# Attention by key chunks of 128, with the leftover 64 keys of two head pairs in one shared slot

## The chip, the cores and the metric

The kernel runs on one core of one Trainium2 chip. The metric is the device time in microseconds (us) of one execution. The engines' short names are those of the profile: PE (matrix multiply, TensorE), PEld (its weight loads), DVE (VectorE), ACT (ScalarE), POOL (GpSimd) and SP (SyncE, which mostly issues DMA transfers).

## The reference

Attention with normalized queries and keys is followed by a feed-forward block with a squared ReLU. There are 8 batches, 12 heads, 448 rows a head and 64 numbers a row; everything is float32.

```python
q_n, k_n = rmsnorm(q, g_q), rmsnorm(k, g_k)          # over the 64 numbers of a row
scores = matmul(q_n, k_n.T) / sqrt(64)
attn = exp(scores - max(scores)); attn = attn / (sum(attn) + 1e-9)
x = matmul(attn, v)                                   # then (B,H,S,D) -> (B*S, H*D): 3584 x 768
h = maximum(x @ w_in, 0)                              # w_in 768 x 2048
out = (h * h) @ w_out                                 # w_out 2048 x 768
```

## The kernel before

**Pairs, chunks and visits.** Two heads make a pair, and their 2 x 64 numbers fill the 128 rows of the array. There are 48 pairs, six to a batch. The 448 keys of a pair are cut into NJ = 4 chunks of 112. For a chunk `weigh` (L312 on) multiplies the chunk's keys with all 448 queries, for each head on its own half of the array's rows (L327). ACT takes the exponential into a tile `wT` (L329), with the key's 1/rms as its scale. `attend` (L366 on) multiplies `wT` with the values, each head on its own half of the array's columns (L372). A visit (`visit`, `weigh_chunks`) attends two chunks of the pair before and weighs two chunks of this pair. So a pair has two visits and a unit of two batches has 24.

**Denominators.** For the first two batches (`alone(i)`) the sums of the weights come from a matmul with ones after each chunk (L379). For the later ones POOL adds the four chunks' weights (`add_up`, L340), and one matmul with ones a pair (`denominators`, L387) sums over the keys. Then DVE inverts (L406) and multiplies (`finish`, L415). The result `xT` is a piece of the transposed x.

**Queries and keys.** `Rows` loads them (L120), squares them on ACT (L133), sums on DVE (L138, L141), takes the power -1/2 on POOL (L147) and scales the queries (L163). For the first 14 pairs PE transposes them (`turn`, L307). For later ones (`in_blocks`) the queries go out to memory and come back in blocks of 32 x 32 (`store_q`, `load_blocks`), and DVE transposes the blocks (L264). Up to batch 1 a row's place in its tile is "(p j)": chunk j holds the rows 4p + j. From batch 2 on the keys and values are "(j p)". `store` writes output rows in the same two orders, so a tile of 128 rows often leaves in pieces.

**Feed-forward part.** It works on units of two batches, with a seven-product scheme for a 2 x 2 block product. `first_products` (L520, 448 columns) makes h; DVE adds (L540), and ACT applies ReLU and square (L541, L542). `second_products` (L572 and L601, 384 columns) makes the output, which DVE adds up in `acc` (L642). The combinations of x that it needs are made by `make_x_forms` (L442) on DVE and POOL, once both batches' pairs are there. The weights are converted piece by piece in the first stage and in unit 0 (`convert`; L710 to L712, L723 to L751).

**Order.** The order in which instructions are issued on every engine is written out by hand (`manual_schedule`). In the first stage (`visit_alone`) attention runs with no feed-forward work between. From then on `ffn(u)` is a generator with a cost for every product, and `run` works through it until a given share is spent; between two such runs stands a visit (`visit_among`). So each unit's feed-forward part has the attention of a later unit between its products. The last unit runs bare. Small jobs wait in `tasks` (DVE) and `pool_tasks` (POOL) and are issued one or two after each product.

**PSUM banks.** There are eight. Scores use banks 0 to 3, two chunks deep; values use bank 4 (4 and 5 in the first two batches). Denominators use 6 and 7 in the first two batches and bank 3 after them. The feed-forward part has 5 to 7.

Of the kernel before, what the change touches and what calls it, by code (L numbers as in the profile page):

```python
# [21 lines left out]
P = 128  # L22


NJ = 4
BY_ROW = "p j"

IN_ORDER = "j p"
# [8 lines left out]
MOST_G = 7.5  # L37


@with_exitstack  # L40
def kernel(
# [19 lines left out]
    CP = q.shape[2] // NJ  # L61
    const = ctx.enter_context(tc.tile_pool(name="const", bufs=1))
    ident = const.tile([P, P], F32, name="ident")
    ones = const.tile([CP, D], F32, name="ones")
    minus_half = const.tile([CP, 1], F32, name="minus_half")
# [4 lines left out]
    with tc.tile_pool(name="early", bufs=1) as early, tc.manual_schedule(engines=ENGINES):  # L70
        for n, g in enumerate((g_q, g_k)):
            nc.scalar.dma_start(g_rows[:, n], g.rearrange("(one d) -> one d", one=1))
        rows.load(0, (nc.sync, nc.scalar))
# [11 lines left out]
        rows.normalize_first(0, early)  # L85
# [5 lines left out]


class Rows:


    def __init__(self, nc, pools, q, k, ones, minus_half):
        self.nc, self.pools, self.qk = nc, pools, (q, k)
        self.ones, self.minus_half = ones, minus_half
        self.B, self.H, self.S, self.D = q.shape
        self.CP = self.S // NJ  # L100
        self.tiles, self.squares, self.ms, self.rr = {}, {}, {}, {}
        self.room = {}

    def go_on(self, io, small):

        other = copy(self)
        other.pools = SimpleNamespace(io=io, small=small)
        other.tiles, other.rr = dict(self.tiles), dict(self.rr)
        return other

    def new_tile(self):
        return self.pools.io.tile([P, 2, 2 * NJ, self.D], F32, name="qk", tag="qk")

    def load(self, i, queues, orders=(BY_ROW, BY_ROW)):
        b, c = divmod(i, self.H // 2)
        self.room[i] = self.new_tile()
        qk = self.room[i][: self.CP]
        for x, rows in enumerate(self.qk):
            for e in range(2):
                queues[x].dma_start(  # L120
                    qk[:, x].rearrange("p (j h) d -> p j h d", h=2)[:, :, e],
                    rows[b, 2 * c + e].rearrange(f"({orders[x]}) d -> p j d", j=NJ),
                )
        self.tiles[i] = qk
        small = self.pools.small
        self.ms[i] = small.tile([self.CP, 2, 2 * NJ], F32, name="ms", tag="ms")
        self.rr[i] = small.tile([self.CP, 2, 2 * NJ], F32, name="rr", tag="rr")

    def square(self, i, x, pool=None):
        squares = (pool or self.pools.io).tile(  # L130
            [self.CP, 2 * NJ, self.D], F32, name="squares", tag=f"squares{x}", bufs=1
        )
        self.nc.scalar.activation(squares, self.tiles[i][:, x], AF.Square)  # L133
        self.squares[i, x] = squares

    def add(self, i, x):
        ms = self.ms[i][:, x]
        self.nc.vector.tensor_reduce(  # L138
            out=ms, in_=self.squares.pop((i, x)), axis=AX.X, op=ALU.add
        )  # L140
        self.nc.vector.tensor_scalar(  # L141
            out=ms, in0=ms, scalar1=1.0 / self.D, scalar2=1e-6, op0=ALU.mult, op1=ALU.add
        )

    def power(self, i, which):
        ms = self.ms[i][:, which].rearrange("p x r -> p (x r)")
        self.nc.gpsimd.tensor_tensor(  # L147
            out=self.rr[i][:, which].rearrange("p x r -> p (x r)"), in0=ms,
            in1=self.minus_half.to_broadcast(list(ms.shape)), op=ALU.pow,
        )  # L150

    def normalize_first(self, i, pool=None):

        for x in range(2):
            self.square(i, x, pool)
            self.add(i, x)
            self.power(i, ds(x, 1))
            if x == 0:
                self.scale(i, x, self.nc.vector)

    def scale(self, i, x, engine):
        qk = self.tiles[i][:, x]
        engine.tensor_tensor(  # L163
            out=qk, in0=qk,
            in1=self.rr[i][:, x, :, None].to_broadcast([self.CP, 2 * NJ, self.D]), op=ALU.mult,
# [4 lines left out]
def program(ctx, tc, rows, v, g_row, ident, moe_w_in, moe_w_out, out, shift):  # L170
# [4 lines left out]
    CP = S // NJ  # L175
# [21 lines left out]
    g = const.tile([P, 1], F32, name="g")  # L197

# [10 lines left out]
    last = len(pairs) - 1  # L209
    values, turned, through = {}, {}, {}  # L210
    weights, sums, dens, xts, forms = {}, {}, {}, {}, {}
    complete = deque()

# [4 lines left out]
    def load_qk(i):  # L218
        if i > last:
            return  # L220

        orders = [IN_ORDER if in_order(i) and not (x == 0 and in_blocks(i)) else BY_ROW for x in range(2)]
        rows.load(i, (nc.sync, nc.sync), orders)
# [3 lines left out]


    def in_order(i):

        return pairs[i][0] > 1 and not shift
# [5 lines left out]
    def room_for_blocks(i, x):  # L237
        return rows.room[i][:, x].rearrange("p r d -> p (r d)")[:, 0:S]

    def store_q(i):  # L240
        through[i] = dram.tile([CP, NJ, 2, D], F32, name="q_rows", tag="q_rows", bufs=2)
        nc.sync.dma_start(
            through[i].rearrange("p j h d -> p (j h d)"),
            rows.tiles[i][:, 0].rearrange("p r d -> p (r d)"),
        )

    def load_blocks(i, x):
        if i > last or not in_blocks(i):
            return
        b, c = pairs[i]  # L250
        by_head = through.pop(i).rearrange("p j h d -> h (p j) d") if x == 0 else None
        for e in range(2):
            source = by_head[e] if x == 0 else rows.qk[1][b, 2 * c + e]
# [15 lines left out]
    def load_v(i):  # L269
        b, c = pairs[i]  # L270
        vt = io.tile([CP, 2, NJ, D], F32, name="vt", tag="vt")
        if in_order(i):
            for e in range(2):
                nc.sync.dma_start(
                    vt[:, e], v[b, 2 * c + e].rearrange(f"({IN_ORDER}) d -> p j d", j=NJ)
                )
        else:
            nc.sync.dma_start(
                vt.rearrange("p h j d -> p h (j d)"),
                v[b, 2 * c : 2 * c + 2].rearrange("h (p j) d -> p h (j d)", j=NJ),  # L280
            )
        values[i] = vt

    def square(i):
        if i <= last:
            for x in range(2):
                rows.square(i, x)

    def normalize(i):

        if i <= last:
            for x in range(2):
                rows.add(i, x)
            rescale(i)

    def rescale(i):
        rows.power(i, ds(0, 2))
# [3 lines left out]
    def turn(i, x):  # L301

        qk = rows.tiles[i][:, x].rearrange("p (j h) d -> p j (h d)", h=2)
        tr = banks[6 - 2 * x + (i - 1) % 2 if i < 2 or alone(i - 2) else 0][:, 0:S]
        dst = att.tile([P, S], F32, name="qT" if x == 0 else "kT")
        for j in range(NJ):
            nc.tensor.transpose(tr[:, ts(j, CP)], qk[:, j], ident[:CP, :CP])  # L307
        if x == 0:
            nc.vector.tensor_scalar(out=dst, in0=tr, scalar1=g, scalar2=None, op0=ALU.mult)  # L309
        else:  # L310
            nc.scalar.copy(dst, tr)
        turned[i, x] = dst  # L312

    def new_weights(i, m):
        for e in range(2):
            weights[i, e, m] = att.tile([CP, S], F32, name="wT", tag="wT", bufs=2 * NJ)

    def weigh(i, m):

        if shift:  # L320
            return weigh_shifted(i, m)
        new_weights(i, m)
        qT, kT = turned[i, 0], turned[i, 1]
        scs = [banks[m % 2 * 2 + e][:CP, 0:S] for e in range(2)]
        for e, sc in enumerate(scs):
            r = ds(e * D, D)
            nc.tensor.matmul(sc, lhsT=kT[r, ts(m, CP)], rhs=qT[r, :], start=True, stop=True)  # L327
        for e, sc in enumerate(scs):
            nc.scalar.activation(  # L329
                weights[i, e, m], sc, AF.Exp, scale=rows.rr[i][:, 1, 2 * m + e : 2 * m + e + 1]  # L330
            )

    def add_up(i, e, m):

        if m == 1:
            sums[i, e] = att.tile([CP, S], F32, name="sum", tag="sum", bufs=2)
            left = weights[i, e, 0]
        else:
            left = sums[i, e]
        nc.gpsimd.tensor_tensor(out=sums[i, e], in0=left, in1=weights[i, e, m], op=ALU.add)  # L340

    def weigh_shifted(i, m):

        if m == 0:
            for n in range(NJ):
                new_weights(i, n)
        qT, kT = turned[i, 0], turned[i, 1]
        for e in range(2):
            r = ds(e * D, D)
            sc = banks[e][:CP, 0:S]  # L350
            nc.tensor.matmul(sc, lhsT=qT[r, ts(m, CP)], rhs=kT[r, :], start=True, stop=True)
            nmax = small.tile([CP, 1], F32, name="nmax", tag="nmax")
            nc.vector.tensor_reduce(out=nmax, in_=sc, axis=AX.X, op=ALU.max, negate=True)
            w = ffn_p.tile([CP, S], F32, name="w", tag="part", bufs=4)
            nc.scalar.activation(w, sc, AF.Exp, bias=nmax)
            tr = banks[2][:CP, 0:S].rearrange("p (n c) -> p n c", n=NJ)
            for n in range(NJ):
                nc.tensor.transpose(tr[:, n, :], w[:, ts(n, CP)], ident[:CP, :CP])
            for n in range(NJ):
                nc.vector.tensor_copy(out=weights[i, e, n][:, ts(m, CP)], in_=tr[:, n, :])  # L360

    def values_bank(i):
        return banks[4 + i % 2 if alone(i) else 4][:, 0:S]

    def sums_bank(i):
        return banks[6 + i % 2 if alone(i) else 3][:, 0:S]  # L366

    def attend(i, m):

        av = values_bank(i)  # L370
        for e in range(2):
            nc.tensor.matmul(  # L372
                av[ds(e * D, D), :], lhsT=values[i][:, e, m, :], rhs=weights[i, e, m],
                start=m == 0, stop=m == NJ - 1,
            )
        for e in range(2):
            wT = weights.pop((i, e, m))
# [630 lines left out]
```

## Time and profile before

The time before is 1500.86 us, the median of 3 runs (1498.45 to 1501.35). The profiled execution's span is 1497.4 us.

| stage (us) | what runs | PE busy | DVE busy | ACT busy | POOL busy |
|---|---|---|---|---|---|
| 0 to 17.48 | start | 5.65 | 5.28 | 5.80 | 5.63 |
| 17.48 to 84 | first stage, mostly batch 0 | 66.52 | 56.08 | 53.55 | 29.81 |
| 84 to 149 | first stage, mostly batch 1 | 62.59 | 50.13 | 42.40 | 28.21 |
| 157.8 to 170.53 | start of unit 0 | 7.30 | 7.19 | 4.42 | 12.73 |
| 209 to 506 | unit 0, attention between | 281.78 | 243.47 | 173.86 | 165.18 |
| 506 to 1226 | units 1 and 2, attention between | 720.00 | 291.32 | 271.65 | 329.15 |
| 1226 to 1497.4 | last unit, bare | 264.97 | 77.98 | 59.33 | 33.85 |

| group | records | mean ns of one |
|---|---|---|
| L520 first products | 1344 | 544 |
| L601, L572 second products | 1344, 256 | 490 to 494 |
| L327 scores | 768 | 569 |
| L372 values | 768 | 550 |
| L379 ones, first two batches | 192 | 539 |
| L387 denominators | 144 | 564 |
| L329 exponentials on ACT | 384 | 635 |

An fp32 matmul leaves two records, each with its weight load. Records of PE overlap, so a mean is longer than the time that one adds; what one adds is read from the chain of waits or from the timeline, as the distance between starts. When a busy time is compared with its stretch, an engine at 100% of the stretch is what bounds it.

### The profile page before, as it was taken

Reading aid. Unit: us, or ns where it says so; the run is one execution under the profiler, and the core shown is the slowest. Engines: PE = TensorE matmul, PEld = TensorE weight load, DVE = VectorE, ACT = ScalarE, POOL = GpSimd, SP = SyncE. Lnnn points to the kernel's source line nnn. Section 1 sums busy time; section 2 is a strip of 40 time slices with the busy share of each in tenths; the row PEclk is TensorE's granted clock in tenths of the full one; section 3 lists DMA queues with packets and bytes.
Section 4 is the critical chain, followed back from the end, with each engine's and each line's share of the span. In section 5 each row is a group of like instructions: output and inputs, shape, how many; then the busy total and the mean of one; then the engine's idle time right before and its main releaser. Section 6 shows DMA issues by size and latency. Waiting matters only on the chain.

```text
span 1497.4 us, 15196 instructions
## 1 busy us (share of the span) xinstructions
PE 1456.1 (97%) x4932; PEld 698.9 (47%) x4932; DVE 753.9 (50%) x1225; ACT 635.2 (42%) x1199; POOL 629.3 (42%) x502
## 2 busy tenths in 40 slices
PE   6999899989899999999999999999999999999998
PEld 2333344444344444545454454545444455555554
DVE  4987558787987742335244453324434251122323
ACT  5776456745547334451423435343342403222130
POOL 4444754563735745344344554534452341020111
PEclk9999999999999999999999999999999999999999
DMA  5565325556556564433525454452543224223122
GB/s 133 156 179 157 74 58 148 175 169 183 146 176 195 181 188 117 127 89 90 158 76 150 128 158 115 97 158 74 152 117 109 69 64 179 84 74 121 37 84 77
DMA packets 287132, 188.08 MB, mean 126 GB/s; under 512 B 252388, under 2 KB 267364, under 8 KB 278852
## 3 DMA queue, kind: packets, MB, share of 16 engines
q1 hardware_dynamic: 285984, 186.45, 42.9%
q8 instruction: 41, 0.67, 0.2%
q10 hardware_dynamic: 1060, 0.57, 0.1%
q14 instruction: 47, 0.39, 0.1%
HBM read 144.57 MB, written 42.40 MB: 125 GB/s over the span
## 4 chain that ended last, share of the span: by engine, by line
PE 89%; DVE 6%; issue 1%; ACT 1%; DMA 1%; POOL 1%; SPq 0%; DVEq 0%; ACTq 0%; POOLq 0%
PE bank L520 32%; PE bank L601 27%; PE bank L327 10%; PE bank L372 10%; PE bank L572 5%; PE bank L379 2%; PE bank L387 2%; DVE xT L406 1%; PE bank L307 1%; ACT wT L329 1%; DVE words L723 1%; DVE acc L642 1%; DMA qk<-in_k_dram 1%; POOL xT L442 1%; DMA qk<-in_q_dram 0%
## 5 line engine op out<-in xcount | busy, mean ns | idle before, releaser
L520 PE MATMUL bank<-xT,in_sb 128*128 128x448 f32 x1344 | 519.2, 544 | 5.4 <-ACT part L527 5.1
L520 PEld LDWEIGHTS bank<-xT,in_sb 128*128 128x128 f32 x1344 | 252.3, 190 | 269.1 <-issue 252.7
L642 DVE TENSOR_TENSOR acc<-acc,bank 128x384 f32<-128x384 f32 x324 | 171.6, 544 | 249.7 <-PE bank L601 174.1
L147 POOL TENSOR_TENSOR rr<-ms,minus_half 112x16 f32<-112x16 f32 (+1 forms) x50 | 140.7, 2813 | 322.6 <-DVE ms L141 322.2
L601 PE MATMUL bank<-out_sb,hid 128*128 128x384 f32 x768 | 269.4, 490 | 5.8 <-DVE acc L642 5.8
L329 ACT ACTIVATE wT<-bank,rr 112x448 f32<-112x448 f32 x384 | 212.1, 635 | 135.5 <-PE bank L327 133.4
L540 DVE TENSOR_TENSOR hid<-bank,part 128x448 f32<-128x448 f32 x128 | 76.9, 622 | 312.6 <-PE bank L520 312.5
L601 PE MATMUL bank<-out_sb,sums 128*128 128x384 f32 x576 | 206.3, 494 | 7.6 <-DVE acc L642 7.4
L601 PEld LDWEIGHTS bank<-out_sb,hid 128*128 128x128 f32 x768 | 144.8, 191 | 115.2 <-DVE acc L642 12.7
L327 PE MATMUL bank<-qT,kT 64*112 64x448 f32 x768 | 175.4, 569 | 1.2 <-DVE qT L309 1.2
L340 POOL TENSOR_TENSOR sum<-sum,wT 112x448 f32<-112x448 f32 x144 | 165.0, 1172 | 26.7 <-ACT wT L329 26.7
L372 PE MATMUL bank<-wT,vt 112*64 112x448 f32 x768 | 168.8, 550 | 2.4 <-ACT words L711 2.4
L541 ACT ACTIVATE hid<-hid 128x448 f32<-128x448 f32 x128 | 73.3, 573 | 208.4 <-DVE hid L540 208.4
L556 POOL TENSOR_TENSOR sums<-hid 128x384 f32<-128x384 f32 x32 | 33.0, 1031 | 294.1 <-ACT hid L542 294.1
L601 PEld LDWEIGHTS bank<-out_sb,sums 128*128 128x128 f32 x576 | 107.7, 191 | 94.4 <-DVE acc L642 14.3
L527 ACT COPY part<-bank 128x448 f32<-128x448 f32 x128 | 67.7, 530 | 140.3 <-PE bank L520 140.3
L406 DVE RECIPROCAL xT<-xT 128x224 f32<-128x224 f32 x72 | 108.6, 1531 | 28.3 <-ACT xT L391 28.3
L138 DVE TENSOR_REDUCE ms<-squares 112x8 f32<-112x512 f32 x96 | 65.3, 680 | 92.2 <-ACT squares L133 92.2
L327 PEld LDWEIGHTS bank<-qT,kT 64*112 64x112 f32 x768 | 63.9, 174 | 101.0 <-issue 87.9
L340 POOL TENSOR_TENSOR sum<-wT 112x448 f32<-112x448 f32 x72 | 82.0, 1159 | 66.4 <-PE bank L387 66.4
L372 PEld LDWEIGHTS bank<-wT,vt 112*64 112x64 f32 x768 | 49.0, 137 | 97.3 <-issue 82.7
L266 ACT ACTIVATE qT<-qT,g 128x448 f32<-128x448 f32 x34 | 22.7, 669 | 165.6 <-DVE qT L264 165.6
(58 smaller groups left out, 1144.0 us busy)
## 6 DMA issues: line engine op xcount, KB each, us to landing
out_sb<-out_forms SPq DMA_DIRECT2D x24, 1536.0 KB, 9.4
in_sb<-in_forms SPq DMA_DIRECT2D x24, 1344.0 KB, 6.2
words<-in_moe_w_in_dram SPq DMA_DIRECT2D x32, 384.0 KB, 3.6
words<-in_moe_w_out_dram SPq DMA_DIRECT2D x32, 384.0 KB, 3.3
out_forms<-out_sb SPq DMA_DIRECT2D x8, 1536.0 KB, 6.9
qk<-in_q_dram SPq DMA_DIRECT2D x96, 112.0 KB, 3.1
in_forms<-in_sb SPq DMA_DIRECT2D x8, 1344.0 KB, 5.9
qk<-in_k_dram SPq DMA_DIRECT2D x94, 112.0 KB, 2.9
```

The lines of the kernel that those rows point to most:

```text
L147: self.nc.gpsimd.tensor_tensor(out=self.rr[i][:, which].rearrange("p x r -> p (x r)"), in0=ms, in1=self.minus_half.to_broadcast(list(ms.sh ...
L327: nc.tensor.matmul(sc, lhsT=kT[r, ts(m, CP)], rhs=qT[r, :], start=True, stop=True)
L329: nc.scalar.activation(weights[i, e, m], sc, AF.Exp, scale=rows.rr[i][:, 1, 2 * m + e : 2 * m + e + 1])
L340: nc.gpsimd.tensor_tensor(out=sums[i, e], in0=left, in1=weights[i, e, m], op=ALU.add)
L372: nc.tensor.matmul(av[ds(e * D, D), :], lhsT=values[i][:, e, m, :], rhs=weights[i, e, m], start=m == 0, stop=m == NJ - 1,)
L406: nc.vector.reciprocal(out=dens[i][:, some], in_=den[:, some])
L520: nc.tensor.matmul(ps, lhsT=w_sb[:, IN.index(left), c, :], rhs=forms[u, c][right], start=first and c == 0, stop=c == NK - 1, skip_group_ch ...
L540: nc.vector.tensor_tensor(out=dst, in0=left, in1=right, op=op)
L541: nc.scalar.activation(dst, dst, AF.Relu)
L572: nc.tensor.matmul(ps, lhsT=flat[a][:, t, ds(NT * P, P)], rhs=w_sb[t][:, 2 * a + half, :], start=(a, t) == parts[0], stop=(a, t) == parts[-1],
L601: nc.tensor.matmul(ps, lhsT=lefts[left][:, t, ts(tt, P)], rhs=w_sb[t][:, OUT.index(right), :], start=first and t == 0, stop=t == 1, skip_g ...
L642: nc.vector.tensor_tensor(out=acc, in0=acc, in1=ps, op=ALU.add)
```

## The change

The keys are cut into NJ = 3 chunks of 128, and the 64 that are left (rows 384 to 447) of two neighbouring pairs share one slot. So two pairs take NG = 7 slots where they took 8 chunks: three of the even pair, the shared one, three of the odd pair. In the shared slot each pair and head has a quarter of the array: scores go to rows by head and columns by pair, values to rows by pair and columns by head. One exponential of 128 x 448 then serves both pairs. A unit has 42 slots in 21 visits, each of which weighs a slot, attends the two of the visit before, and weighs another. Rows stand in their natural order everywhere, so output tiles leave in one piece.

What goes with it:

- Scores rotate over banks 0 to 2. Values use bank 4 for even pairs and 3 for odd ones. Denominators after batch 1 and late transposes use bank 2; early transposes have bank 5.
- In the first stage a slot is weighed two slots before it is attended (LAG = 2), and loads, squares, sums and transposes are set on slot numbers by a table of events.
- `denominators` is called halfway between two visits instead of inside one.
- `begin_forms` makes the combinations of x for unit 0 pair by pair while batch 1 is attended.
- Pair 1 is loaded at the very start on POOL's queue, and pairs 2 and 3 right after; two rooms hold two pairs each.
- Squares and sums have 8 groups of 64 for even pairs (with the shared rows) and 6 for odd ones, where all had 8.
- POOL still adds weights three times a pair and head; the shared slot's halves are added on 64 partitions each.

The diff, cut to its core:

```diff
-NJ = 4
+NJ = 3
+NG = 2 * NJ + 1
...
+    slots = [
+        (i + (j > NJ), j - (NJ + 1) * (j > NJ))
+        for i in range(0, len(pairs), 2) for j in range(NG)
+    ]
+    LAG = 2
...
+    def weigh(n):
+        i, m = slots[n]
+        scs = [banks[(2 * n + e) % 3][:, 0:S] for e in range(2)]
+        for p in pairs_of(n):
+            some = ds(p % 2 * LASTS, LASTS) if m == NJ else ds(0, P)
+            keys = ds(m * P, LASTS if m == NJ else P)
+            for e, sc in enumerate(scs):
+                r = ds(e * D, D)
+                nc.tensor.matmul(
+                    sc[some], lhsT=turned[p, 1][r, keys], rhs=turned[p, 0][r, :],
+                    start=True, stop=True,
+                )
         for e, sc in enumerate(scs):
             nc.scalar.activation(
-                weights[i, e, m], sc, AF.Exp, scale=rows.rr[i][:, 1, 2 * m + e : 2 * m + e + 1]
-            )
+                new_weights(n, e), sc, AF.Exp, scale=rows.rr[i][:, 1, 2 * m + e : 2 * m + e + 1]
+            )
...
     def values_bank(i):
-        return banks[4 + i % 2 if alone(i) else 4][:, 0:S]
+        return banks[4 - i % 2][:, 0:S]
 
     def sums_bank(i):
-        return banks[6 + i % 2 if alone(i) else 3][:, 0:S]
+        if shift:
+            return banks[3 + i % 2][:, 0:S]
+        return banks[6 + i % 2 if alone(i) else 2][:, 0:S]
...
+    def attend(p, m, key, first, last):
+        some = ds(p % 2 * LASTS, LASTS) if m == NJ else ds(0, P)
         for e in range(2):
             nc.tensor.matmul(
-                av[ds(e * D, D), :], lhsT=values[i][:, e, m, :], rhs=weights[i, e, m],
-                start=m == 0, stop=m == NJ - 1,
-            )
+                values_bank(p)[ds(e * D, D), :],
+                lhsT=lasts[p // 2][some, e, :] if m == NJ else values[p][:, m, e, :],
+                rhs=weights[key, e][some], start=first, stop=last,
+            )
...
+    def begin_forms(c):
+        if c < NK:
+            b11, b12, t1 = xts.pop((0, c)), xts.pop((1, c)), new_x()
+            less(nc.vector, t1, b12, b11)()
+            forms[0, c] = {"11": b11, "T1": t1, "T3": b12}
+            return
+        c -= NK
+        b21, b22, t2, t4 = xts.pop((0, c + NK)), xts.pop((1, c + NK)), new_x(), new_x()
+        some = forms[0, c]
+        less(nc.vector, t2, b22, some["T1"])()
+        less(nc.gpsimd, some["T3"], b22, some["T3"])()
+        less(nc.gpsimd, t4, t2, b21)()
+        some.update({"21": b21, "22": b22, "T2": t2, "T4": t4})
...
+    def visit(n):
+        run_tasks()
+        now = [s for s in (2 * n, 2 * n + 1) if s < len(slots)]
...
+        for s in now[:1]:
+            weigh_and_add(s)
+        while attending and attending[0] <= 2 * n - 2:
+            attended.update(attend_slot(attending.popleft()))
+        for s in now[1:]:
+            weigh_and_add(s)
...
+    def halfway(n):
+        do_events(2 * n + 1)
...
+        for i in [i for i in summed if summed[i] == n - 1]:
+            del summed[i]
+            denominators(i)
```

## The prediction

> **What bounds the kernel now.** I read the page first (busy shares and slices), then the waits of the matmul engine, then busy time by stage, last the chain of waits in a stretch of the interleaved stage.
>
> ```profile
> PE 1456.1 (97%) x4932; PEld 698.9 (47%) x4932; DVE 753.9 (50%) x1225; ACT 635.2 (42%) x1199; POOL 629.3 (42%) x502
> PE   6999899989899999999999999999999999999998
> PE 89%; DVE 6%; issue 1%; ACT 1%; DMA 1%; POOL 1%; SPq 0%; DVEq 0%; ACTq 0%; POOLq 0%
> ```
>
> PE is busy everywhere and makes 89% of the chain. So only three things count: PE time taken off, PE time added, and gaps put in or closed. The gaps of now:
>
> ```profile
> PE bank L601 <- DVE acc L642: 13.3, 12, 2.3
> PE bank L520 <- ACT part L527: 5.1, 1, 5.1
> ```
>
> ```profile
> 157.80:170.53 12.73, 7.30 (x21) 3.26 (x19) 7.19 (x7) 4.42 (x9) 12.73 (x11) 0.98 0.49 100
> ...
> 209.00:506.00 297.00, 281.78 (x908) 130.47 (x907) 243.47 (x392) 173.86 (x339) 165.18 (x128) 0.99 0.59 168
> 506.00:1226.00 720.00, 720.00 (x2398) 346.56 (x2397) 291.32 (x477) 271.65 (x504) 329.15 (x271) 1.00 0.43 120
> ```
>
> The first two lines are waits: who, for whom, us in total, times, longest. The others are stretches: from:to, length, then busy us of PE, PEld, DVE, ACT, POOL, the granted clock, DMA. From 506 to 1226 us PE has no gap. In unit 0 of the feed-forward part (209 to 506) it loses 15 us, nearly all to VectorE, which is 82% busy there. At 157.8 to 170.5, where unit 0 begins, it loses 5.4 us to a queue of GpSimd subtractions (L442, busy throughout).
>
> Now the price of attention, from the chain of waits (start, length, what):
>
> ```profile
> 672.11 5.36 PE bank L572 x16
> 677.46 6.45 PE bank L601 x20
> 683.91 1.65 PE bank L372 x8
> 685.57 1.69 PE bank L327 x8
> 687.26 10.52 PE bank L601 x32
> 697.78 0.90 PE bank L387 x4
> 698.68 1.50 PE bank L372 x8
> 700.18 1.69 PE bank L327 x8
> ```
>
> A chunk, both heads, is 4 records (two per fp32 matmul). L372 costs 1.50 for two chunks when L387, of the same array shape, is ahead: **0.75 us a chunk**, for two matmuls side by side. The rest is the price of changing the array's shape: 1.65 - 1.50 = 0.15 into L372, 0.90 - 0.75 = 0.15 into L387, 1.69 - 1.50 = 0.19 into L327, and back into the feed-forward 0.20 (L601 without a change is 6.45/20 = 0.3225 each; 10.52 - 32 x 0.3225 = 0.20; L572 the same). One visit of now costs 0.15 + 1.50 + 0.19 + 1.50 + 0.20 = 3.54 us, 15% of it shape changes.
>
> **The Trainium skill.** "TensorEngine Tiling (Array Packing)", Tiling Modes: 64x64 gives four independent tiles, and changing the mode, not just the tile, drains the engine. The trace agrees on the drain (0.15 to 0.20 us above) and shows two tiles at full concurrency; four it doesn't show. "TensorE: Matmul & The Clock Gate", Part 3: concurrent tiles start about 4 ns apart, and weight loads of other tiles overlap. Here the two heads of L327 start some 7 ns apart, so four tiles should cost near 0.77 us, not 1.5. "DMA: Bandwidth & Descriptors", SWDGE vs HWDGE: a copy issued by GpSimd has its descriptors written in software, first byte about 1 us against 0.6; before issues none from there.
>
> **The change, part by part.**
>
> *Fewer chunks.* Two pairs take 7 slots, not 8. Of 192 QK chunks and 192 AV chunks, 24 each go; of the 48 ones-chunks (L379, first two batches), 6. At 0.75: 54 x 0.75 = **40.5 us off**, if the shared slot's four matmuls run together. 128 columns or rows in place of 112 cost nothing: time follows the 448 moving columns. What it costs back is in the order.
>
> *Interleaved stage, shape changes.* A visit now has QK, AV AV, QK between feed-forward work: 0.19 + 0.15 + 0.19 + 0.20 = 0.73 of changes, where it was 0.54. Before: 70 full visits x 0.54 and two AV-only x 0.35 = 38.5. After (unit = 21 visits; 44 of 168 slots are weighed before unit 0, so 124 slots in 62 visits, and two AV-only): 62 x 0.73 + 0.7 = 46.0. The 18 shared slots' AV is 64x64 beside a 128x64 neighbour: one more change, 18 x 0.17 = 3. **+10.5.**
>
> *Denominators.* 24 of 36 pairs had L387 right before L372: 0.75 and no extra change. Now all 36 stand alone in the middle of feed-forward work: 0.15 + 0.75 + 0.20 = 1.10. 24 x 0.35 = **+8.4.** (The 12 of unit 0 stood alone already.)
>
> *Interleaved chunks off.* QK 140 to 124 slots, AV 144 to 126: 34 x 0.75 = 25.5. Net of the stage: -25.5 + 10.5 + 8.4 = **-6.6 us.** Most of the gain is eaten by shape changes.
>
> *First stage (two batches, no feed-forward work).* QK 52 to 44, AV with ones 48 to 42: 8 x 0.75 + 6 x 1.5 = 15 off. But the shape changes at each slot, 3.5 times a pair, not 2: 12 x 1.5 x 0.34 = +6.1; transposes move 128 columns, not 112: about +1.5. Net **-7.4**.
>
> *begin_forms.* The combinations for unit 0 are made pair by pair in batch 1 instead of all at its start. That takes away the 5.4 us gap and the slowed clock after it (the next stretch shows 0.96 granted): **-7**. The cost: six VectorE subtractions of 1.07 us (L442) land in a first stage where VectorE is 77 to 84% busy, next to the conversions of weights. Nothing but slack hides them.
>
> *Waits added.* Scores rotate over three banks instead of four, so the second head of a visit's second QK needs the exponential of its first slot. That one is due 0.94 + 1.65 + 0.19 = 2.8 us after the visit begins. ACT works in order; where a visit follows the last product of a group (P7), its queue holds four L541/L542 first:
>
> ```profile
> 1194.08 0.97 PE L387 MATMUL bank<-sum,ones 112*64 112x448 f32 x4
> 1194.91 0.58 ACT L541 ACTIVATE hid<-hid 128x448 f32<-128x448 f32 x1 [2.45 <-DVE hid L540]
> ...
> 1196.59 0.58 ACT L542 ACTIVATE hid<-hid 128x448 f32<-128x448 f32 x1
> ```
>
> They end 3.1 us after the visit begins; the exponential (0.635, L329) makes it 3.7, and PE, with all of the feed-forward queued behind, stands for 1 us. By the code's costs two visits a unit follow P7: 6 us, and one or two more where VectorE is late in unit 0 (one such queue today clears 6.5 us after its visit began), 2 us. Bank 3 of now is both a score bank and the denominators', which makes L327 2.09 for 1.69 in eight visits of units 1 and 2; that goes, -3. Sum **+5**; bounds 0 and +15.
> In the first stage transposes have one bank, 5, and scores three: between 0 and +10; I take **+3**.
>
> *Start.* Pair 1's loads come early (now, in the timeline, PE stands 3.6 us until 17.48 for pair 1), but twelve loads of pairs 2 and 3 and the weights are queued on SyncE ahead of the first v; at about 0.62 us an issue (two of L120 take 1.24) v leaves near 18 us, not 15.9, and its use waits. The extra copies of the leftover rows delay the first squares by about 1 us. **+1**, bounds -3 and +4.
>
> *At no cost.* ACT exponentials 384 to 336 (30 us off), squares, sums of squares and powers an eighth fewer: hidden under PE from 506 us on; in the first stage they pay for part of the new subtractions. GpSimd additions stay 216. Output rows leave in one piece: hidden. The smaller descriptors of the q round trip: DMA is 43% busy, and loads have ten slots of lead.
>
> Sum: -6.6 - 7.4 - 7 + 5 + 3 + 1 = -12, so 1500.9 - 12 = **1489**.
>
> **Rivals.**
> *Waits eat it (slower side).* VectorE near its limit in batch 1 and the three banks make PE wait 15 us more than I took, and unit 0 adds a few: about -12 + 20 = 1509. For it: VectorE at 82% in unit 0, work in bursts (1.2 to 2.3 us for operations that take 0.6 alone, next to GpSimd). Against: weights are attended two slots late, and from 506 us VectorE is only 40% busy. Chance 0.18.
> *Quarters don't overlap.* The shared slot costs 1.5: the 40.5 come back, 1529. Against: columns (L372) and rows (L327) each overlap fully today, and a quarter only combines them. Chance 0.07.
> *Much of it pays.* No new waits (-8), the start gains 3 instead of losing 1 (-4), unit 0's VectorE gaps shrink by 10: 1489 - 22 = 1467. For it: less VectorE work per pair. Against: the conversions, which make these gaps, are untouched. Chance 0.18.
>
> **How the numbers follow.** Forecast (1480 to 1498) 0.57. The range runs to the two middle rivals, 1467 to 1510, and leaves out the quarter case and a tail. Faster by over 0.2% (below 1497.9): 0.47 of the forecast's 0.57 and the 0.18 above, 0.65; within 0.2%: 0.11; slower: 0.24.
>
> **What would show it.** Right: four L327-like records per normal slot in 0.75 plus change, eight in about 0.77 in the shared slot; QK twice a visit, each with its own 0.19; denominators at 1.1; no gap where unit 0 starts; between 506 and the last unit PE still without gaps except short ones before the second QK, ended by ACT. Wrong: a shared slot at 1.5; PE in the first stage waiting for VectorE or ACT; score matmuls waiting more than 1 us in most visits; or shape changes cheaper than 0.15 once the work around them differs, which would leave up to 15 us more gain.

## The result and the profile after

The changed kernel takes **1519.72 us** (median of 4; 1519.22 to 1525.42) against 1500.25 before: a ratio of 1.014 (95% interval 1.0113 to 1.0166), so 19 us slower, where 12 us faster was forecast.

The page of the changed kernel (busy times, PE by slices, the chain's shares):

```profile
PE 1466.0 (97%) x4932; PEld 680.2 (45%) x4932; DVE 754.0 (50%) x1225; ACT 613.6 (40%) x1151; POOL 614.0 (40%) x508
PE   6998999988999999999999999999999999999997
PE 79%; DVE 9%; issue 4%; ACT 3%; DMA 2%; POOL 2%; SPq 0%; DVEq 0%; ACTq 0%; POOLq 0%
```

ACT has 48 operations less, POOL and DVE are much as they were. PE is still busy nearly everywhere, but makes only 79% of the chain, down from 89%: more of the time is decided by other engines. The waits of PE over the whole run (who, for whom, us in total, times, longest), cut to those that answer to the ones of before:

```profile
PE bank L365 <- ACT wT L370: 12.6, 8, 3.5
PE bank L445 <- DMA vt<-in_v_dram: 7.6, 4, 3.3
...
PE bank L713 <- DVE acc L754: 4.9, 4, 2.3
```

L365 is QK (L327 of before), L445 AV (L372), L713 the second products (L601), L632 the first (L520), L481 the denominators (L387). QK's wait for an exponential is new. AV's wait for v had come once before, on a line of the kernel before that names another engine:

```profile
89.87 0.97 PE L372 MATMUL bank<-wT,vt 112*64 112x448 f32 x4 [2.41 <-ACT words L711]
```

The v of this matmul was issued at 83.03 us and landed at 89.74, just before PE went on; in two later runs of the kernel before with small edits the same stop is put down to v (2.8 and 2.3 us). Now there are four such stops. The wait of the second products for VectorE fell from 13.3 to 4.9, and the wait of the first products at the start of unit 0 is gone.

Stage by stage, with a stage's start at its first product's record (us):

| | first stage | unit 0 | unit 1 | unit 2 | last unit |
|---|---|---|---|---|---|
| before | 157.8 | 382.4 | 351.1 | 344.3 | 261.9 |
| changed | 161.6 | 396.0 | 351.8 | 344.5 | 263.5 |
| of it QK, before | 54.4 | 40.6 | 42.2 | 37.1 | |
| of it QK, changed | 53.6 | 67.2 | 43.5 | 36.4 | |

(QK is the time from each of its records' starts to the next record's start on PE.) Most of the loss is in unit 0, and in unit 0 it is QK, 26.6 us more; the rest of unit 0 is 13 us shorter. Busy PE doesn't show this well, since records that stand in a wait or run at half clock count as busy; the stretch does (length, busy PE, PEld, DVE, ACT, POOL, granted clock, DMA):

```profile
161.60:557.70 396.10, 376.98 (x1203) 169.18 (x1201) 291.02 (x462) 204.03 (x392) 211.48 (x169) 0.97 0.55 149
557.70:909.50 351.80, 351.38 (x1171) 162.29 (x1169) 145.91 (x236) 131.83 (x242) 160.10 (x134) 1.00 0.45 123
```

(The 1.6 us that the last unit grew by come after its last product; its matmuls take the same time as before.)

The chain in a stretch of unit 1 where nothing is late shows the visit as it was meant (start, length, what):

```profile
587.75 0.95 PE bank L365 x4
588.70 1.65 PE bank L445 x8
590.35 0.95 PE bank L365 x4
591.30 6.96 PE bank L632 x18
598.27 0.90 PE bank L481 x4
599.17 4.71 PE bank L684 x14
603.88 0.91 PE bank L365 x8
604.79 1.65 PE bank L445 x8
606.45 0.95 PE bank L365 x4
```

The shared slot's eight records at 603.88 take 0.91: **the four quarters run together**, 0.75 and 0.16 for the change of shape. (Its four first records start within 0.02 us of each other.) QK is 0.75 + 0.20 each time, twice a visit, and the denominators 0.90 on the way in, all as forecast.

Now unit 0. The timeline of the changed kernel from 368 us (start, busy us, engine, line, operation, tiles, shapes, count, idle time before and what ended it):

```profile
368.09 1.72 PE L445 MATMUL bank<-wT,vt 128*64 128x448 f32 x8
...
369.22 1.55 DVE L500 RECIPROCAL xT<-xT 128x224 f32<-128x224 f32 x1
...
369.74 1.02 PE L365 MATMUL bank<-qT,kT 64*128 64x448 f32 x2
370.80 0.62 DVE L509 TENSOR_TENSOR xT<-bank,xT 128x448 f32<-128x448 f32 x1
371.34 0.61 DVE L652 TENSOR_TENSOR hid<-bank,part 128x448 f32<-128x448 f32 x1
...
371.99 0.58 ACT L653 ACTIVATE hid<-hid 128x448 f32<-128x448 f32 x1 [4.86 <-DVE hid L652]
...
373.08 2.42 ACT L370 ACTIVATE wT<-bank,rr 128x448 f32<-128x448 f32 x4
...
373.75 1.02 PE L365 MATMUL bank<-qT,kT 64*128 64x448 f32 x2 [2.99 <-ACT wT L370]
...
374.69 3.71 PE L632 MATMUL bank<-xT,in_sb 128*128 128x448 f32 x5
```

Read upward from the end. QK's second head stands 3 us for an exponential. ACT could have done that one earlier, but in its order a ReLU of the products comes first, and that waited 4.86 us for VectorE. VectorE was at conversions, a reciprocal and a product before it came to L652. PE's bank wait joins two queues, ACT's and VectorE's, that are filled mostly by other work. And L632 then needs 0.74 us a record where 0.375 is usual: for 3.4 us the granted clock (the third number from the end) is at half:

```profile
375.13:378.55 3.42, 3.42 (x6) 1.69 (x5) 0.00 (x0) 0.37 (x1) 3.34 (x3) 0.50 1.05 170
```

### The profile page after: what moved, and what is told of

Read it like the earlier page. It is cut to its first block, busy times and chain, and to the rows that moved or that the text cites. A ratio compares the mean times of both kernels' runs of the same rounds, so it can differ in the third digit from the quotient of the medians.

```text
span 1517.4 us, 15217 instructions
## 1 busy us (share of the span) xinstructions
PE 1466.0 (97%) x4932; PEld 680.2 (45%) x4932; DVE 754.0 (50%) x1225; ACT 613.6 (40%) x1151; POOL 614.0 (40%) x508
## 3 DMA queue, kind: packets, MB, share of 16 engines
q1 hardware_dynamic: 306784, 186.44, 43.5%
## 4 chain that ended last, share of the span: by engine, by line
PE 79%; DVE 9%; issue 4%; ACT 3%; DMA 2%; POOL 2%; SPq 0%; DVEq 0%; ACTq 0%; POOLq 0%
PE bank L632 31%; PE bank L713 26%; PE bank L365 8%; PE bank L445 7%; PE bank L684 5%; DVE xT L500 2%; PE bank L481 2%; DMA vt<-in_v_dram 1%; PE bank L454 1%; DVE acc L754 1%; DVE words L827 1%; POOL rr L177 1%; DVE hid L652 1%; DMA words<-in_moe_w_in_dram 1%; ACT hid L653 1%
## 5 line engine op out<-in xcount | busy, mean ns | idle before, releaser
L632 PE MATMUL bank<-xT,in_sb 128*128 128x448 f32 x1344 | 523.6, 546 | 0.4 <-DVE acc L754 0.4
L632 PEld LDWEIGHTS bank<-xT,in_sb 128*128 128x128 f32 x1344 | 252.6, 191 | 266.1 <-issue 249.4
L370 ACT ACTIVATE wT<-bank,rr 128x448 f32<-128x448 f32 x336 | 194.2, 628 | 234.3 <-PE bank L365 215.6
L713 PE MATMUL bank<-out_sb,hid 128*128 128x384 f32 x768 | 274.3, 494 | 6.0 <-DVE acc L754 4.6
L652 DVE TENSOR_TENSOR hid<-bank,part 128x448 f32<-128x448 f32 x128 | 76.7, 620 | 397.9 <-PE bank L632 397.9
L713 PE MATMUL bank<-out_sb,sums 128*128 128x384 f32 x576 | 205.0, 490 | 0.7 <-ACT acc L752 0.4
L365 PE MATMUL bank<-qT,kT 64*128 64x448 f32 (+1 forms) x768 | 191.8, 591 | 14.0 <-ACT wT L370 12.6
L713 PEld LDWEIGHTS bank<-out_sb,hid 128*128 128x128 f32 x768 | 145.7, 192 | 119.0 <-DVE acc L754 8.8
L177 POOL TENSOR_TENSOR rr<-ms,minus_half 128x16 f32<-128x16 f32 (+3 forms) x50 | 126.4, 2528 | 173.8 <-DVE ms L171 163.5
L388 POOL TENSOR_TENSOR sum<-sum,wT 128x448 f32<-128x448 f32 (+1 forms) x144 | 163.9, 1155 | 51.4 <-ACT wT L370 47.8
L388 POOL TENSOR_TENSOR sum<-wT 128x448 f32<-128x448 f32 x72 | 83.9, 1175 | 202.6 <-PE bank L481 201.5
L653 ACT ACTIVATE hid<-hid 128x448 f32<-128x448 f32 x128 | 73.3, 573 | 215.3 <-DVE hid L652 215.3
L713 PEld LDWEIGHTS bank<-out_sb,sums 128*128 128x128 f32 x576 | 107.6, 190 | 85.8 <-issue 8.2
L445 PE MATMUL bank<-wT,vt 128*64 128x448 f32 x576 | 135.2, 567 | 7.6 <-DMA vt<-in_v_dram 7.6
L365 PEld LDWEIGHTS bank<-qT,kT 64*128 64x128 f32 (+1 forms) x768 | 54.7, 173 | 124.2 <-issue 80.7
L684 PE MATMUL bank<-out_sb,hid 128*128 128x384 f32 x256 | 89.3, 496 | 0.0
L445 PEld LDWEIGHTS bank<-wT,vt 128*64 128x64 f32 x576 | 33.7, 137 | 97.9 <-issue 84.6
L654 ACT ACTIVATE hid<-hid 128x448 f32<-128x448 f32 x128 | 73.8, 577 | 4.1
```

Of the source, the lines that this page charges most:

```text
L177: self.nc.gpsimd.tensor_tensor(out=self.rr[i][:, first : first + number, 0 : self.count(i)], in0=ms, in1=self.minus_half[:, :, None].to_br ...
L365: nc.tensor.matmul(sc[some], lhsT=turned[p, 1][r, keys], rhs=turned[p, 0][r, :], start=True, stop=True,)
L370: nc.scalar.activation(new_weights(n, e), sc, AF.Exp, scale=rows.rr[i][:, 1, 2 * m + e : 2 * m + e + 1])
L388: nc.gpsimd.tensor_tensor(out=all_three[0], in0=all_three[1], in1=all_three[2], op=ALU.add)
L445: nc.tensor.matmul(values_bank(p)[ds(e * D, D), :], lhsT=lasts[p // 2][some, e, :] if m == NJ else values[p][:, m, e, :], rhs=weights[key, ...
L632: nc.tensor.matmul(ps, lhsT=w_sb[:, IN.index(left), c, :], rhs=forms[u, c][right], start=first and c == 0, stop=c == NK - 1, skip_group_ch ...
```

## The experiments

The theory: with three score banks the second QK of a visit needs the first slot's exponential, and in unit 0 ACT is too late for that. The rivals: VectorE bounds unit 0 in any case, so the wait would only show elsewhere; or what costs is the shape changes.

**The second slot weighed half a visit later, in unit 0 only**

```diff
-        scs = [banks[(2 * n + e) % 3][:, 0:S] for e in range(2)]
+        scs = [banks[e if among and first else (2 * n + e) % 3][:, 0:S] for e in range(2)]
...
         for s in now[1:]:
-            weigh_and_add(s)
+            if not (among and first):
+                weigh_and_add(s)
...
     def halfway(n):
+        if among and first and first_end < n and 2 * n + 1 < len(slots):
+            weigh_and_add(2 * n + 1)
```

> The changed kernel, except that in unit 0 a visit's second slot is weighed halfway to the next visit, and both slots use score banks 0 and 1 there, so that no score matmul waits for an exponential of the same visit. Theory 'three banks' (ACT is late in unit 0, and the second QK waits for the first slot's exponential): QK in unit 0 falls from 67 us to about 45, its waits on ACT from 33 us to under 5; 22 more changes of the array's shape cost some 4 us; unit 0 from 396 us to about 376, the whole about 1500. Rival 'VectorE bounds unit 0': the wait only moves to the products' matmuls, unit 0 stays above 390 us, the whole at 1514 or more.

Measured: 1495.69 us, ratio to before 0.9962 (0.9948 to 0.9977): the loss is gone, though unit 0 has one score bank less here than in the change. The five runs spread from 1490.9 to 1496.4 us, and the stages given here are those of the run at 1490.9. Unit 0 took 367.4 us for 396.0, QK in it 44.8 for 67.2. The first and second products got 5.8 us shorter too, since the slow clock went with the stops: the granted clock of unit 0 rose from 0.97 to 1.00. What QK's weight loads waited for, in unit 0 of the changed kernel and then of this one (us, times):

```profile
  ACT wT L370: 33.5, 21
```

```profile
  ACT wT L370: 1.4, 2
```

The rival would have kept unit 0 above 390 us. VectorE's busy time there is the same in both (291.0 and 290.4 us); it was late, not the bound.

**Less work for VectorE in unit 0, in both kernels**

```diff
             high = words[n][:, :, 1]
-            nc.vector.tensor_scalar(
+            if n < ahead:
+                nc.vector.tensor_scalar(
...
-            nc.vector.scalar_tensor_tensor(
+            if n < ahead:
+                nc.vector.scalar_tensor_tensor(
...
-            nc.vector.tensor_tensor(out=bits, in0=bits, in1=low, op=ALU.add)
+                nc.vector.tensor_tensor(out=bits, in0=bits, in1=low, op=ALU.add)
```

> The changed kernel with a lighter conversion of weights in unit 0: for its 48 pieces three of the four VectorE operations are left out (clamp, sign, add of the low part; some 85 us of VectorE), so the weights of blocks 1 to 3 are not the reference's. ScalarE's part and the transfers stay. Theory 'ACT is late because VectorE is': QK in unit 0 falls from 67 us to about 45 and unit 0 from 396 to about 373, since the queue of ACT clears in time although the three banks stay; about 1497. Rival 'ACT is late because it waits for the words' transfers': QK's waits stay above 15 us, the whole above 1508.

> The kernel before with the same lighter conversion (the same three operations left out, so the weights of blocks 1 to 3 are not the reference's). It has four score banks, so only its own waits for VectorE in unit 0 (13 us, L601 for acc) can go: unit 0 from 382 us to about 369, about 1487. If the changed kernel gains some 22 us and this one 13, the loss in unit 0 needs both the late VectorE and the three banks.

Measured: 1483.11 and 1483.36 us, both at a ratio of 0.9895 to before. The changed kernel gains 37 us from it and the kernel before 16. Unit 0 takes 361.5 us in the changed kernel and 365.2 in the kernel before. So its loss depends on VectorE being late: with VectorE's queue light, three banks cost little there (QK's weight loads wait 7.4 us for L370, not 33.5). The totals are equal because the changed kernel's first stage is still 2.9 us longer. I had expected 1497 and 1487. Both gained more: VectorE lost 104 us of work in the changed kernel's unit 0, not 85, and the feed-forward matmuls there got 16 and 17 us shorter, since their own waits for VectorE went, and most of the slow clock with them.

The rival was that ACT waits for the transfers of the words (the weights as they are loaded, before conversion). As the whole cause it is refuted, for QK's waits fell below 15 us. But the two are not taken apart by this run: ACT's waits for the words fell too, from 14.8 us to 4.8. In unit 0 of the changed kernel ACT waited 46.5 us for L652 and 14.8 for the words, and the longest stop of PE was of the second kind:

```profile
312.04 0.55 ACT L814 ACTIVATE words<-words 128x384 f32<-128x384 f32 x1 [4.45 <-DMA words<-in_moe_w_in_dram]
```

```profile
314.16 1.85 PE L365 MATMUL bank<-qT,kT 64*128 64x448 f32 x2 [3.55 <-ACT wT L370]
```

SyncE issued this transfer at 305.46 us, right after VectorE had freed the buffer (L855 ended at 305.39), and it landed 6.5 us later, where 3.6 is usual.

**v loaded two slots earlier in the first stage**

```diff
-        event(begin_of(i), load_v, i)
+        event(max(begin_of(i) - (2 if begin_of(i) < 2 * first_end + 2 else 0), 0), load_v, i)
```

> The changed kernel, except that in the first stage v is loaded two slots earlier (four slots ahead of its use, not two); same buffers. Theory 'v has half the lead it had': AV's three waits for v's transfer (3.9, 2.4 and 2.4 us apart where 0.5 is usual) go, with the slow clock after them; first stage from 161.6 us to about 154, the whole about 1512. Rival 'the first stage is bound by VectorE and GpSimd in any case': the waits turn into waits of transposes or of QK; first stage above 159, the whole at 1517 or more.

Measured: 1510.70 us, 9.0 less; the first stage 153.4 for 161.6. The longest of the four waits for v in the changed kernel, from the timeline of the DMA queue and of PE (SPq is SyncE's queue, its time is issue and waiting):

```profile
77.95 10.91 SPq L800 DMA_DIRECT2D words<-in_moe_w_out_dram  x2
88.95 0.92 SPq L316 DMA_DIRECT2D vt<-in_v_dram  x2
```

```profile
92.18 2.19 PE L445 MATMUL bank<-wT,vt 128*64 128x448 f32 x4 [3.34 <-DMA vt<-in_v_dram]
```

v stands behind a load of weights that waits for its buffer, which VectorE frees (L855, up to 10.1 us). Before, v stood a pair ahead of its use in the order of the code, some 10 us; now two slots, 5 to 6. With four slots the same queue reads as below, and no wait for v is left on PE:

```profile
80.93 0.92 SPq L316 DMA_DIRECT2D vt<-in_v_dram  x2
81.93 1.26 SPq L324 DMA_DIRECT2D vl<-in_v_dram  x2
91.42 0.35 SPq L800 DMA_DIRECT2D words<-in_moe_w_out_dram  x1
```

**Both edits**

> The changed kernel with both edits: the second slot of unit 0's visits weighed halfway, and v loaded two slots earlier in the first stage. If both theories hold, their gains add: about 1493, faster than before by 0.4%. If VectorE bounds either stage, 1505 or more.

Measured: 1479.17 us, 0.9855 (0.984 to 0.987). The gains of the two edits, 24.0 and 9.0, make 40.5 together, more than their sum. Unit 0 is 28.7 us shorter here and 28.6 with the first edit alone, in its run at 1490.9; the 24.0 is that of its median, 4.8 us higher. The rest is the first stage, which varied by some 3 us between kernels that are the same there (150.2 here, 153.3 in a later one, 153.4 with v's edit alone).

**begin_forms alone, in the kernel before**

```diff
-        if b % 2 and c >= NK:
+        if b == 1 and not shift:
+            begin_forms(c)
+        elif b % 2 and c >= NK:
             complete.append((b // 2, c - NK))
```

> The kernel before with begin_forms alone: the combinations of x for unit 0 are made pair by pair in batch 1. Theory of the prediction: the 5 us gap at the start of unit 0 and the slow clock after it go, 7 us less, about 1493. Rival: VectorE in batch 1 has no room for six more operations, so the first stage grows by as much; about 1500.

Measured: 1498.52 us, 0.9992 (0.9985 to 0.9999): hardly anything. The subtractions were gone from the start of unit 0, and PE stood there as before. The waits from 157 to 175 us tell why:

```profile
ACT qT L266 <- DVE qT L264: 7.6, 1, 7.6
...
DVE qT L264 <- DMA qk<-q_rows: 4.8, 1, 4.8
PE bank L540 <- ACT part L547: 4.2, 1, 4.2
```

(L540 and L547 are L520 and L527 of the kernel before.) Behind the subtractions stood a second wait of almost the same length. The first products need ACT's copies; ACT stands at the scaling of pair 14's queries, which wait for the transposition, and that for the round trip of the queries through memory. Then come squares of rows whose load stood behind that round trip in SyncE's queue; the last of it landed at 170.45 us, and PE went on at 171.66. Unit 0 got 2.0 us shorter, the first stage 2.6 longer, which is within what it varies by. So the rival, that VectorE has no room in batch 1, is not excluded.

**begin_forms undone, in the best version**

```diff
-        if b == 1:
-            begin_forms(c)
-        elif b % 2 and c >= NK:
+        if b % 2 and c >= NK:
             complete.append((b // 2, c - NK))
```

> The same without begin_forms: the combinations for unit 0 are made at its start by make_x_forms, as in the kernel before. Theory of the prediction: the gap at the start of unit 0 (5 us and the slow clock after it) comes back, 7 us, partly paid back by a first stage with six VectorE operations less; about 1482. Rival: the gap before was due to the round trip of queries and the loads queued behind it, which the table of events has moved; then begin_forms is worth nothing here, about 1477.

Measured: 1483.98 us against 1476.23 with it, 7.7 more, all in unit 0's first products (unit 0: 373.9 for 366.2). Here, where the queries are fetched by slot numbers well ahead, the subtractions are PE's only wait at the start of unit 0, and with the slow clock after it the forecast's 7 us are right:

```profile
PE bank L630 <- DVE xT L532: 4.4, 3, 2.2
```

**The second slot half a visit later in all units**

```diff
-        scs = [banks[e if among and first else (2 * n + e) % 3][:, 0:S] for e in range(2)]
+        scs = [banks[e if among else (2 * n + e) % 3][:, 0:S] for e in range(2)]
```

(and the same condition in the other two places.)

> The changed kernel with every visit's second slot weighed halfway to the next visit, in units 0, 1 and 2, on score banks 0 and 1. Beside the version that does so in unit 0 alone (1495.7) this adds a change of shape into QK and one back in 40 visits in place of one into QK: about 0.2 us each, 8 us, against 2 to 3 us of score waits in units 1 and 2 that go. Theory of the price of shape changes: units 1 and 2 grow by 5 to 7 us together, about 1501. Rival 'what costs in a visit is not the change of shape but waits': units 1 and 2 the same or shorter.

Measured: 1489.35 us; units 1 and 2 took 349.9 and 344.1 for 351.8 and 344.5. They got 2.3 us shorter, not longer, as the rival had it. The price of a change of shape was right in my expectation, and two counts were wrong. Where denominators are due halfway they now stand right behind QK and share its way back, 23 times:

```profile
603.36 0.95 PE bank L365 x4
604.32 0.90 PE bank L481 x4
605.22 6.65 PE bank L713 x20
```

That is 40 x 0.20 - 23 x 0.20 = +3.4 us, not 8. Against it, the waits of the second QK in units 1 and 2 of the changed kernel were 6.1 us, not 2 to 3 (what six of its 39 visits take above the usual 0.95 or 0.91), and none is left: -2.7 together.

**Denominators inside the visit** (`divide` holds what `halfway` does for a pair's denominators, now half a visit earlier; `sums_bank` returns `den_bank[0]` after batch 1)

```diff
         for s in now[:1]:
             weigh_and_add(s)
+        if not first:
+            den_bank[0] = banks[(4 * n + 2) % 3]
+            divide(n)
+            den_bank[0] = banks[2]
```

> The faster version (second slot halfway in unit 0, v two slots earlier; 1479.2), and in units 1 and 2 the denominators' matmul inside the visit, between the first QK and AV, in the one score bank that is free then, instead of alone in the middle of feed-forward work. It takes away a change of shape into it and one back, 0.35 us each for 24 pairs: 8 us less, about 1471. Rival: PE waits there for GpSimd's sums or the second QK waits for the copy of the denominators: no gain or a loss.

Measured: 1486.79 us, 7.6 worse than without. Units 1 and 2 grew by 3.3 and 1.9 us (and the first stage, which the edit doesn't touch, by 3.1). The rival was right; what the saved changes of shape bring is more than lost again:

```profile
PE bank L483 <- POOL sum L388: 11.1, 2, 5.7
```

(L483 is the denominators' matmul here.) Half a visit earlier GpSimd's sums are twice not ready, and PE stands some 5.5 us each time.

**The best version: the second slot halfway in all units, v two slots earlier**

> The second slot of every visit weighed halfway in units 0, 1 and 2, and v loaded two slots earlier in the first stage. Units 1 and 2 were 2.3 us shorter with the edit in all units than in unit 0 alone, so 1479.2 - 2 = about 1477. If the two edits don't add, about 1480.

Measured: **1476.23 us, 0.9844 (0.9831 to 0.9858)**: 23 us faster than before and 43 faster than the change as it was made. PE now makes 88% of the chain:

```profile
PE 1444.1 (98%) x4932; PEld 668.0 (45%) x4932; DVE 752.5 (51%) x1225; ACT 608.9 (41%) x1151; POOL 615.9 (42%) x508
...
PE 88%; DVE 5%; issue 2%; ACT 1%; DMA 1%; POOL 1%; SPq 0%; DVEq 0%; ACTq 0%; POOLq 0%
```

## Why the prediction was wrong

**What failed is the term "Waits added", +5 with bounds 0 and +15.** The mechanism was named: three banks, the second QK, ACT's order, the 2.8 us in which the exponential is due. The size was wrong, above all for unit 0, which had 4 of the 8 us: 2 for visits after P7 and 2 for "one or two more where VectorE is late". Measured: in unit 0 the edit that removes the wait took 28.6 us off, though it adds some 2 us of shape changes (22 more, 12 of them shared with denominators); so the wait cost about 30 us there. In units 1 and 2 it cost 6.1, where 4 were taken.

Three things made it large in unit 0. The second QK was held up in 11 of 23 visits, by 23 us in all. In seven of them, 12 us, ACT's last wait before the exponential was for L652 on VectorE, which is 73% busy in this stage; in one, 1.3 us, it was for transposed queries, also from VectorE. In three, 9 us, the splits of weights on ACT (L814 to L816) had waited for their words, for which the prediction took nothing. And five stops of 2.1 to 3.6 us in this unit, three of them of QK, were each followed by half clock: 20.5 us of it in all, for 10.2 before and none with the edit. I had counted the slow clock for the start of unit 0 and not here.

The trace of before had the evidence. Of the 24 visits of its unit 0, ACT's queue cleared 3.1 to 3.3 us after the visit began in five, and 6.5 us after it in three, at 281.65, 378.21 and 477.56, once in each block that converts weights:

```profile
281.65 1.72 PE L372 MATMUL bank<-wT,vt 112*64 112x448 f32 x8
...
286.94 0.58 ACT L541 ACTIVATE hid<-hid 128x448 f32<-128x448 f32 x1 [2.09 <-DVE hid L540]
287.55 0.58 ACT L542 ACTIVATE hid<-hid 128x448 f32<-128x448 f32 x1
288.03 2.19 ACT L329 ACTIVATE wT<-bank,rr 112x448 f32<-112x448 f32 x4
```

With four banks PE did not wait for this exponential. I took such a queue for a rare case. Priced as the prediction priced the others, these eight visits make 3 x 4.3 + 5 x 0.9 = some 17 us, an estimate, before any slow clock.

**A wait that was missed: v.** "Start" priced v's late issue only for the first use. That v's lead had been halved for every pair of the first stage was in the code (`load_v` at `begin_of(i)`, attended two slots later), and the waits for DVE on SyncE's queue ahead of v were in the profile. It cost 8.2 us of the first stage: the profiled kernels with v's late issue have 161.4 to 164.5 us there, those with the early one 150.2 to 153.4. Without it the stage takes 153.4 us, 4.4 less than before; forecast, with its waits and the start, were 3.4 less.

**What held.** The quarters overlap (0.91 in the shared slot). The price of shape changes came out within 0.01 us: 0.15 into AV and into denominators, 0.20 into QK, 0.16 into a quarter, 0.20 back. So "most of the gain is eaten by shape changes" holds: units 1 and 2 together grew by 0.9 us, and without their 6.1 us of waits they would have gained 5. begin_forms is worth 7.7 us in the best version and next to nothing in the kernel before. The forecast hadn't seen the condition, which by the waits is the earlier fetch of queries; the fetch was not moved on its own. The 13.3 us that the second products waited for VectorE in unit 0 fell to 4.9. A part of that is no gain: with QK's waits taken away it is 7.1 to 7.5, so PE had stood in QK instead. What made the rest of the fall was not tried.

**The rivals.** "Waits eat it", 1509 at a chance of 0.18, was the right one, and still 10 us too low. It looked for the waits in batch 1 and gave unit 0 only a few. "Much of it pays", 1467, counted on no new waits; with the waits taken away, the best version came to 1476, between it and the forecast.

**What stays open.** How much of the 30 us would go if only the words came earlier was not tried: the trace puts 9 of 23 us of held-up QK behind them, but the lighter conversion frees their buffers earlier too. Nor was it tried whether four score banks, with the visit's order as it is, would do as well as the later slot.

## What to carry to other kernels

When a change takes away a buffer, write down for each reuse who must have finished, on which engine, and what stands ahead of it in that engine's order; then price it with the worst queue that the trace shows, not the usual one. An engine that is 40% busy over the run, ACT here, delivered an exponential 7.1 us after its visit began where it was due at 2.8. When instructions of one array shape are cut into smaller groups, count the changes of shape: 0.15 to 0.20 us each ate most of what seven slots in place of eight had brought. And a wait that is removed may only uncover one of nearly the same length behind it, as begin_forms did in the kernel before.

## What the runs showed of the hardware

- A stop of PE has a tail. After the 3 us stop at 370.8 us of the changed kernel the granted clock was 0.50 for 3.4 us, and the first products' records took 0.74 us where 0.375 is usual. By estimate that makes a stop of 3 us cost 3 + 3.4/2 = 4.7. The Trainium skill tells of this half rate in "TensorE: Matmul & The Clock Gate", Part 1, after an idle window of about 3.4 us. Here shorter stops were enough: half clock followed five stops in unit 0 of the changed kernel, for 3.4 us each and once for 6.8, and four of the five lasted 2.1 to 3.2 us. The length alone doesn't decide it: the stop of 2.4 us that ended at 89.87 us of the kernel before had no slow clock behind it.
- Four quarters of 64 x 64 in fp32 run side by side with no loss that the trace shows: eight records in 0.75 us beside the 0.16 of the change, the same 0.75 as four records of half the array.
- A change between a quarter shape and a half shape costs about what one between halves does, 0.16 us beside 0.15: AV of a visit with the shared slot takes 1.81 us, without it 1.65.
